# Row maxima spread by one bf16 matmul, raw weights of a block in one tile, and loads and sums of the next chunk tied elsewhere in an attention and FFN kernel

## The chip, the cores and the metric

The kernel runs on one core of a Trainium2 chip. The metric is the device time of one execution in microseconds (us). The kernel before was timed three times: 1032.73, 1033.56 and 1032.63 us, a median of 1032.73 us.

## The reference

Windowed causal attention with a linear bias per head, and behind it a feed-forward network (FFN) on all tokens; q and k come in multiplied by 8:

```python
# q, k, v: 8 batches, 8 heads, 576 positions, 64 numbers; float32
scores = scale * np.matmul(q, k.transpose(0, 1, 3, 2))          # scale = 1/8
bias = slopes[:, None, None] * (-np.abs(rel).astype(np.float32))[None, :, :]
mask = (rel >= 0) & (rel < window)                               # window = 128
attn = softmax(np.where(mask, scores + bias[None], -1e9))
x = np.matmul(attn, v)                  # then heads side by side: 4608 tokens x 512
h = x @ w_in                            # 512 x 2048
g = np.where(h >= 1, h, np.where(h <= -1, 0.0, (h + 1) ** 2 / 4.0))
return g @ w_out                        # 2048 x 512
```

`w_in` and `w_out` are float64; the kernel gets them as pairs of 32-bit words and makes float32 of them itself.

## The kernel before

**Tiling.** The 4608 tokens go in 12 chunks of 384 (`CH`), three blocks of 128 each. In a chunk the 8 heads are 4 pairs, so that there are 48 pairs; pair p belongs to chunk p // 4. Chunks 0 and 1 (`c < LIGHT`) have float32 attention, one head after the other (`scores`, `weights_t`, `values`). Chunks from 2 on have it in split fp16: each float32 operand becomes a high and a low half (ACT makes the high one, DVE the low one: `split_qk` L367/L368, `split_v` L424/L425), and three products replace one (`scores_of_pair` L453, `values_of_pair` L557). The FFN of a chunk has 16 blocks fc of 128 hidden units: `layer1` is 12 fp16 matmuls of 384 columns (L585 to L587), `layer2` 9 of 512 columns (L616 to L618; in chunk 0 three in float32, L613). Between the two ACT (L592, L601), DVE (L593, L594) and POOL (L602) make the quadratic unit and its two halves.

**Scales.** A split needs a scale made of the greatest absolute value over a whole tensor. Each engine row (partition) first has its own maximum or sum. To take the maximum over the 128 partitions, `spread` lets POOL multiply a 128x128 identity by that column (L152), a float32 matmul with a matrix of ones turns the diagonal into 128 equal rows (L157), and DVE takes the maximum along the row (L159) and makes scale and inverse (L162 to L170). That happens 19 times: `m_i0` to `m_i15` for the blocks of `w_in`, `m_x0` and `m_x1` for v of chunks 0 and 1, `m_o` for all of `w_out`. For chunks 2 to 11, `level` and `scale_all` do it for two columns at once: POOL L335 twice, one float32 matmul of 256 columns, L341. A float32 matmul is issued as two passes, which is why the profile counts 32 `m_i` and 20 `m`.

**Weights.** Block fc of `w_in` and of `w_out` arrives in two raw tiles (`rawi`, `rawo`, three of each) by two DMAs on ACT's queue. `float32_of` makes float32 of each: ACT scales the high words (L176) and the low words (L177), DVE shifts (L178) and adds (L179). `convert_in` has the row maximum `rows_i` made behind it (L198), `convert_out` a sum (L222). Three blocks are converted in the attention of chunk 0, the others in its FFN, three blocks ahead of their use.

**Loads and sums of a pair.** From pair 8 on `load_all(p)` brings q, k and v by DMAs on SP's queue. q and k of pairs from 12 on go into one of five tiles in turn (`p % 5`, taken over from the raw weights), v into one of six (`vn`). `reach_of(p)` makes the row maximum of v on DVE (L384, `rows<-vn`) and the sums of the absolute values of q and of k on ACT (L318, `junk<-qk`); when a chunk's four pairs have theirs, `level` and `scale_all` make the chunk's scales, on which `split_qk` of its first pair waits.

**The order.** The attention is a list of `segments`, the FFN a list of its own; of the first so many are emitted after each half of an FFN block that the attention of chunk c + 1 lies in the FFN of chunk c. A scheduler then orders each engine's instructions, by dependences and a simulated time. `behind(instructions, f)` asks that what f emits stand behind the named instructions; it orders instructions of the same engine only. In each turn p of the loop at the end of the list there are, in this order:

```python
reach_of(p + 4); scores_of_pair(p, (0, 1)); level(c + 1)   # level: last pair of a chunk
scores_of_pair(p, (2,)); split_v(p); values_of_pair(p - 1)
scale_all(c + 1)                                           # last pair of a chunk
weights_t(2 * p); split_qk(p + 1) and load_all(p + 5); weights_t(2 * p + 1)
```

Of the kernel before, what the change touches and what calls it, by code (L numbers as in the profile page):

```python
# [20 lines left out]
def windowed_attention_then_ffn(  # L21
# [83 lines left out]
    for m in range(H):  # L105
# [8 lines left out]
    G.affine_select(out=rel, in_=rel, pattern=[[-1, 2 * P]], base=P, channel_multiplier=1,  # L114
                    compare_op=ALU.is_ge, fill=NEG)

    sums = const.tile([P, 2, NQB, 2], F32, name="sums")
    G.memset(sums, 1.0e-9)

# [12 lines left out]
            G.memset(t[:D, 1], 0.0)  # L132


    ones = const.tile([P, P], F32, name="ones")
    G.memset(ones, 1.0)
# [11 lines left out]

    def spread(name, rows):

        diag[name] = ap1.tile([P, P], F32, name=f"d_{name}", tag="d", bufs=2)
        G.tensor_scalar(diag[name], ident, rows, None, ALU.mult)  # L152

    def scale_of(name, s, i):

        b = bank(f"m_{name}")[:, :P]
        T.matmul(b, ones, diag.pop(name), start=True, stop=True)  # L157
# [11 lines left out]
    def float32_of(w, name, out=None):

        low, high = w[..., 0], w[..., 1]
        f = stg.tile([P] + list(w.shape[1:-1]), F32, name=f"f_{name}", tag="stg")
        fi = f.bitcast(I32)


        S.activation(high.bitcast(F32), high.bitcast(F32), AF.Prelu, scale=2.0 ** -112, alpha=2.0 ** 32)  # L176
        S.activation(low, low.bitcast(U32), AF.Copy, scale=2.0 ** -29)  # L177
        V.tensor_scalar(fi, high, 3, None, ALU.logical_shift_left)  # L178
        V.tensor_tensor(fi if out is None else out.bitcast(I32), fi, low, ALU.add)  # L179
        return f  # L180

    raw = {}

    def fetch_weights(fc):
        w1 = rawp.tile([P, NCC, P, 2], I32, name=f"rawi{fc}", tag=f"rawi{fc % 3}")
        S.dma_start(w1, wi32[:, 2 * fc * P:2 * (fc + 1) * P].rearrange("(c p) (f w) -> p c f w", p=P, w=2))

        w2 = rawp.tile([P, DM, 2], I32, name=f"rawo{fc}", tag=f"rawo{fc % 3}")
        S.dma_start(w2, wo32[fc * P:(fc + 1) * P, :].rearrange("p (f w) -> p f w", w=2))
        raw[fc] = (w1, w2)  # L190

    wide = {}

    def convert_in(fc):
        f = wide[fc] = wp.tile([P, NCC, P], F32, name=f"f_i{fc}", tag="f_i", bufs=3)
        float32_of(raw[fc][0], f"i{fc}", out=f)
        rows = column(f"rows_i{fc}", "rows")
        V.tensor_reduce(rows, f.rearrange("p c f -> p (c f)"), X, ALU.max, apply_absolute_value=True)  # L198
# [9 lines left out]
    def split_in(fc):  # L208
        if fc > 1:
            fall_in(fc)  # L210
        f, s1 = wide.pop(fc), s_in[:, fc:fc + 1]
        t = wi[fc] = wp.tile([P, 2, NCC, P], F16, name=f"wi{fc}", tag=f"wi{fc}")
# [5 lines left out]

    def convert_out(fc):
        wf[fc] = wp.tile([P, DM], F32, name=f"wf{fc}", tag=f"wf{fc}")  # L220
        float32_of(raw[fc][1], f"o{fc}", out=wf[fc])
        S.activation(junk, wf[fc], AF.Abs, accum_out=rows_o[:, fc:fc + 1])  # L222

    def scale_out(stage):
# [56 lines left out]
    def load_qk(p):  # L281
# [9 lines left out]
        for j, r in enumerate(lo_rows):  # L291
            DMA.dma_start(kr[r, j, :n], k[g * P + j * D:g * P + (j + 1) * D, (c + 1) * CH - n:(c + 1) * CH])

    def load_all(p):

        c, g = divmod(p, NPAIR)
        n = CH + before(c) * P
        if c == LIGHT:
            t = wp.tile([P, 2 * CH + P], F32, name=f"qk_{p}", tag=f"wo{NPAIR + g}")
        else:  # L300
            tag = ("rawi0", "rawi1", "rawi2", "rawo0", "rawo1")[p % 5]
            t = rawp.tile([P, 2 * CH + P], F32, name=f"qk_{p}", tag=tag)
# [17 lines left out]
    def level(c):  # L320

        rq, rk = tops.pop((c, "q")), tops.pop((c, "k"))
        iq, t = column(f"i_q{c}", "i_q", n=NPAIR), column(f"t{c}", "t", n=NPAIR)
        top = column(f"tt{c}", "tt", n=2)
        s_q[c], s_k[c] = column(f"s_q{c}", "s_q", n=NPAIR), column(f"s_k{c}", "s_k", n=NPAIR)
        V.tensor_scalar(iq.bitcast(I32), rq.bitcast(I32), 0x7F800000, None, ALU.bitwise_and)
        V.tensor_scalar(iq, iq, 2.0 ** -60, 1.0 / TOP, ALU.max, ALU.mult)
        V.reciprocal(s_q[c], iq)
        V.tensor_tensor(iq, iq, qscale, ALU.mult)
        V.tensor_tensor(t, rk, iq, ALU.mult)  # L330
        V.tensor_reduce(top[:, 0:1], t, X, ALU.max)
        V.tensor_reduce(top[:, 1:2], tops.pop(c)[:, :NPAIR], X, ALU.max)
        d = diag[c] = ap1.tile([P, 2, P], F32, name=f"d_{c}", tag="qr")
        for a in range(2):
            G.tensor_scalar(d[:, a], ident, top[:, a:a + 1], None, ALU.mult)  # L335
        tops[c, "i"] = iq

    def scale_all(c):

        b = bank(f"m_{c}")[:, :2 * P]  # L340
        T.matmul(b, ones, diag.pop(c).rearrange("p a w -> p (a w)"), start=True, stop=True)  # L341
# [11 lines left out]
        if "t" not in rels:  # L353
            rels["t"] = rawp.tile([P, NQB, 2 * P], F32, name="rels", tag="rawo2")
        rels[c] = rels["t"][:, c % 2], rels["t"][:, 2]
# [87 lines left out]
    def scores_of_pair(p, blks):  # L443
# [191 lines left out]
    for m in range(M1):  # L635
# [9 lines left out]
        if m >= 2:  # L645
            part["e"] = [[lambda m=m: values(m - 2)]]
        if odd:
            part["v"] = [[lambda p=p: load_v(p + 4)]] if p < NPAIR else []
            part["v"] += [[lambda x=x: load_all(x)] for x in {5: (8, 9), 6: (10,), 7: (11,)}.get(p, ())]
# [14 lines left out]
    for p in range(M1 // 2, NP):  # L664
        c, g = divmod(p, NPAIR)
        new = p + NPAIR < NP
        if new:
            segments.append([lambda p=p: reach_of(p + NPAIR)])
        segments.append([lambda p=p: scores_of_pair(p, (0, 1))])
        if new and g == NPAIR - 1:  # L670
            segments.append([lambda c=c: level(c + 1)])
        segments.append([lambda p=p: scores_of_pair(p, (2,))])
        segments.append([lambda p=p: split_v(p)])
        if p > M1 // 2:
# [6 lines left out]
        segments.append(([lambda p=p: split_qk(p + 1)] if p + 1 < NP else []) + ([lambda p=p: load_all(p + 5)] if p + 5 < NP else []))  # L681
# [129 lines left out]
```

## Time and profile before

| | |
|---|---|
| median of three runs | 1032.73 us |
| the profiled execution | 1030.51 us |
| its span in the profile | 1028.3 us |
| mean granted TensorE clock | 0.979 |
| instructions in the span | 17951 |

The span runs from the first to the last instruction of the profiled execution; 2.2 us of that execution lie outside it, and the execution itself is 2.2 us below the median. PE is TensorE's matmuls, PEld its weight loads, DVE VectorE, ACT ScalarE, POOL GpSimd, SP the queue that issues loads and stores. A group of instructions reads: line, engine, operation, tiles written and read, shapes, count, then busy time in us and the mean of one in ns, then idle time of the engine ahead of them and what released it. The chain is followed back from the last instruction to whatever released each step.

### The profile page before, as it was taken

How to read it: one execution, taken by the hardware profiler on the slowest of the kernel's cores; microseconds unless marked ns; L12 is line 12 of the kernel's file. 1: busy time of each engine (PE TensorE's matmuls, PEld its weight loads, DVE VectorE, ACT ScalarE, POOL GpSimd, SP SyncE). 2: the span in 40 equal slices, each digit the busy share in tenths (PEclk: the TensorE clock that was granted, in tenths of full speed). 3: DMA queues.
4: the chain of work that ended last, by engine and by line, in shares of the span. 5: the costliest groups of instructions: out<-in, count | busy, mean ns of one | idle time of the engine just before them, and what ended most of it. 6: DMA issues, size and time to landing. Idle time of an engine off the chain costs nothing.

```text
span 1028.3 us, 17951 instructions
## 1 busy us (share of the span) xinstructions
PE 975.1 (95%) x6218; PEld 548.8 (53%) x6218; DVE 742.2 (72%) x2128; ACT 618.2 (60%) x1547; POOL 374.7 (36%) x479
## 2 busy tenths in 40 slices
PE   7579999997899899899999999999999999999998
PEld 7446554554455455455555555555555555555554
DVE  5789889887767677777777777777777867775322
ACT  4678878665756655655755765765755755654332
POOL 5332211334344323433433433433434434334221
PEclk9889999999799999999999999999999999999999
DMA  8445442002101101201211201111101100000000
GB/s 258 159 154 168 160 142 85 1 11 73 52 22 57 57 24 35 69 30 39 68 40 40 74 24 47 57 30 57 60 29 57 50 2 1 32 1 1 32 1 31
DMA packets 53275, 59.88 MB, mean 58 GB/s; under 512 B 3520, under 2 KB 42432, under 8 KB 53184
## 3 DMA queue, kind: packets, MB, share of 16 engines
q1 hardware_dynamic: 42432, 41.96, 13.0%
q10 hardware_dynamic: 10752, 16.78, 4.8%
q8 instruction: 49, 0.80, 0.3%
q14 instruction: 42, 0.34, 0.1%
HBM read 49.28 MB, written 9.44 MB: 57 GB/s over the span
## 4 chain that ended last, share of the span: by engine, by line
PE 81%; DVE 8%; DMA 4%; ACT 3%; issue 2%; POOL 1%; ACTq 0%; SPq 0%; DVEq 0%; POOLq 0%
PE h L585 11%; PE h L587 11%; PE h L586 11%; PE acc L616 11%; PE acc L617 11%; PE acc L618 11%; PE s L453 5%; PE x L557 4%; PE p L497 3%; DMA vn<-in_v_dram 2%; PE acc L613 2%; PE x L536 1%; DVE g L593 1%; ACT z L478 1%; DVE g L594 1%
## 5 line engine op out<-in xcount | busy, mean ns | idle before, releaser
L602 POOL TENSOR_TENSOR gl<-g,gh 128x384 f16<-128x384 f32 x176 | 164.8, 936 | 394.1 <-ACT gh L601 375.9
L593 DVE SCALAR_TENSOR_TENSOR g<-u,half 128x384 f32<-128x384 f32 x176 | 121.0, 689 | 178.1 <-ACT u L592 167.9
L616 PE MATMUL acc<-wo,gh 128*128 128x512 f16 x528 | 200.0, 380 | 0.4 <-ACT wo L238 0.4
L617 PE MATMUL acc<-wo,gh 128*128 128x512 f16 x528 | 200.3, 379 | 0.0
L618 PE MATMUL acc<-wo,gl 128*128 128x512 f16 x528 | 197.0, 379 | 0.0
L601 ACT CAST gh<-g 128x384 f16<-128x384 f32 x176 | 89.7, 509 | 177.3 <-DVE g L594 124.7
L592 ACT ACTIVATE u<-h,shift,fall 128x384 f32<-128x384 f32 x176 | 116.4, 664 | 88.9 <-PE h L587 88.2
L478 ACT ACTIVATE z<-z,nmax 128x256 f32<-128x256 f32 (+2 forms) x288 | 137.7, 479 | 35.5 <-DVE nmax L476 34.8
L585 PE MATMUL h<-xh,wi 128*128 128x384 f16 x448 | 146.4, 328 | 3.7 <-DVE g L594 3.7
L587 PE MATMUL h<-xh,wi 128*128 128x384 f16 x448 | 147.4, 329 | 1.3 <-DVE wi L214 1.3
L586 PE MATMUL h<-xl,wi 128*128 128x384 f16 x448 | 147.2, 328 | 0.0
L476 DVE CUSTOM_DVE_ANT_0 z<-s,rels,z_of 128x256 f32<-128x256 f32 (+2 forms) x240 | 98.4, 459 | 26.8 <-PE s L453 26.4
L594 DVE SCALAR_TENSOR_TENSOR g<-h,gain,g 128x384 f32<-128x384 f32 x176 | 107.8, 614 | 3.8
L585 PE MATMUL h<-x,wi 128*128 128x384 f16 x320 | 105.3, 331 | 4.4 <-ACT x L566 3.1
L586 PEld LDWEIGHTS <-wi 128*128 128x128 f16 x768 | 75.7, 99 | 62.2 <-issue 9.2
L585 PEld LDWEIGHTS <-wi 128*128 128x128 f16 x768 | 75.5, 98 | 62.1 <-issue 6.6
L586 PE MATMUL h<-x,wi 128*128 128x384 f16 x320 | 105.9, 331 | 0.2 <-DVE x L567 0.2
L587 PE MATMUL h<-x,wi 128*128 128x384 f16 x320 | 105.9, 331 | 0.0
L587 PEld LDWEIGHTS <-wi 128*128 128x128 f16 x768 | 75.7, 99 | 54.6 <-issue 4.2
L512 POOL TENSOR_SCALAR_AFFINE_SELECT lu<-lu 128x768 f16<-128x768 f16 x80 | 72.5, 914 | 71.0 <-DVE lu L510 56.7
L618 PEld LDWEIGHTS <-gl 128*128 128x128 f16 x528 | 51.5, 98 | 58.6 <-issue 1.1
L616 PEld LDWEIGHTS <-gh 128*128 128x128 f16 x528 | 51.6, 98 | 52.0 <-issue 2.2
(154 smaller groups left out, 1555.4 us busy)
## 6 DMA issues: line engine op xcount, KB each, us to landing
out_dram<-o SPq DMA_DIRECT2D x36, 256.0 KB, 2.1
rawi<-in_moe_w_in_dram ACTq DMA_DIRECT2D x16, 512.0 KB, 3.7
rawo<-in_moe_w_out_dram ACTq DMA_DIRECT2D x16, 512.0 KB, 4.7
vn<-in_v_dram SPq DMA_DIRECT2D x32, 256.0 KB, 3.0
qk<-in_q_dram SPq DMA_DIRECT2D x40, 192.0 KB, 3.0
qk<-in_k_dram SPq DMA_DIRECT2D x28, 256.0 KB, 3.5
vn<-in_v_dram SPq DMA_DIRECT2D x16, 192.0 KB, 2.7
qk<-in_k_dram SPq DMA_DIRECT2D x12, 192.0 KB, 2.8
```

What stands on the lines that cost most here:

```text
L476: V.tensor_tensor_reduce(out=z[:, i, c0:], in0=pt[:, n, c0:], in1=r[:, c0:], op0=ALU.add, op1=ALU.min, scale=factor, scalar=3.0e38, accum_ ...
L478: S.activation(z[:, i, c0:], z[:, i, c0:], AF.Exp, bias=nmax[:, i:i + 1], scale=-1.0, accum_out=sm[:, i, 0:1])
L585: T.matmul(ph, wi[fc][:, 0, cc, :], xh, start=(cc == 0), stop=False)
L586: T.matmul(ph, wi[fc][:, 0, cc, :], xl, start=False, stop=False)
L587: T.matmul(ph, wi[fc][:, 1, cc, :], xh, start=False, stop=(cc == NCC - 1))
L592: first = S.activation(u, ph, AF.Relu, bias=shift[c] if c else quarter, scale=fall[c][:, col])
L593: V.scalar_tensor_tensor(g, u, half[c] if c else 0.5, u, ALU.min, ALU.mult)
L594: last = V.scalar_tensor_tensor(g, ph, gain[c][:, col] if c else fall[c][:, col], g, ALU.mult, ALU.max)
L602: G.tensor_tensor(gl, g, gh, ALU.subtract)
L616: T.matmul(a, gh[:, ts], wo[fc][:, 0], start=first, stop=False)
L617: T.matmul(a, gh[:, ts], wo[fc][:, 1], start=False, stop=False)
L618: T.matmul(a, gl[:, ts], wo[fc][:, 0], start=False, stop=last)
```

## The change

1. **Spreading a row maximum.** `spread` and `level` make no diagonals any more, they only keep the column. `across` (new) issues one bf16 matmul of 128 columns for each column: the weights are the upper 16 bits of the column, read 128 times over with a stride of zero, and the moving operand is a bf16 identity, which POOL copies once at the start in place of the `ones`. The maximum is only used through its exponent.
2. **Raw weights.** A block's two halves have one tile `raw` (three in turn), by the same two DMAs. `unfold` runs ACT once over the high words of both halves and once over the low words (128x1024 each), in `convert_in`; `float32_of` is one DVE instruction for a half, a shift and an or (L192 after), without a temporary tile.
3. **Six lasting halves.** q and k of pairs from 12 on go to `two[p // 2 % 3][:, p % 2]`, three tiles allocated once with two halves each, in place of five tiles in turn. The scaled distances (`rels`) have a constant tile `near` of their own, one set in place of two in turn.
4. **Turn of a pair.** `load_all(p + 5)` stands at the head of turn p, as a segment of its own, no longer behind `split_qk(p + 1)`; `reach_of(p + 4)` stands behind the first scores and is tied by `behind` to their last matmul. `load_v` and `load_all` of the first chunks are tied to `done_t`, which holds instructions of DVE, ACT and POOL.

```diff
     def spread(name, rows):
-        diag[name] = ap1.tile([P, P], F32, name=f"d_{name}", tag="d", bufs=2)
-        G.tensor_scalar(diag[name], ident, rows, None, ALU.mult)
+        diag[name] = rows
+
+    def across(b, rows):
+        r = rows.bitcast(BF16)
+        for a in range(rows.shape[1]):
+            T.matmul(b[:, a * P:(a + 1) * P], r[:, 2 * a + 1:2 * a + 2].broadcast_to([P, P]), ident16, start=True, stop=True)
...
-        T.matmul(b, ones, diag.pop(name), start=True, stop=True)
+        across(b, diag.pop(name))
...
-        S.activation(low, low.bitcast(U32), AF.Copy, scale=2.0 ** -29)
-        V.tensor_scalar(fi, high, 3, None, ALU.logical_shift_left)
-        V.tensor_tensor(fi if out is None else out.bitcast(I32), fi, low, ALU.add)
-        return f
...
+    def unfold(fc, which=slice(0, 2)):
+        low, high = raw[fc][:, which, :, 0], raw[fc][:, which, :, 1]
         S.activation(high.bitcast(F32), high.bitcast(F32), AF.Prelu, scale=2.0 ** -112, alpha=2.0 ** 32)
+        S.activation(low, low.bitcast(U32), AF.Copy, scale=0.9375 * 2.0 ** -29)
+
+    def float32_of(fc, a, out):
+        V.scalar_tensor_tensor(out.bitcast(I32), raw[fc][:, a, :, 1], 3, raw[fc][:, a, :, 0], ALU.logical_shift_left, ALU.bitwise_or)
...
     def convert_in(fc):
-        f = wide[fc] = wp.tile([P, NCC, P], F32, name=f"f_i{fc}", tag="f_i", bufs=3)
-        float32_of(raw[fc][0], f"i{fc}", out=f)
+        f = wide[fc] = wp.tile([P, DM], F32, name=f"f_i{fc}", tag="f_i", bufs=3)
+        unfold(fc)
+        float32_of(fc, 0, f)
...
     def load_all(p):
-            tag = ("rawi0", "rawi1", "rawi2", "rawo0", "rawo1")[p % 5]
-            t = rawp.tile([P, 2 * CH + P], F32, name=f"qk_{p}", tag=tag)
+            i = p // 2 % 3
+            if i not in two:
+                two[i] = rawp.tile([P, 2, 2 * CH + P], F32, name=f"qk_{p}", tag=f"raw{i}")
+            t = two[i][:, p % 2]
...
-        d = diag[c] = ap1.tile([P, 2, P], F32, name=f"d_{c}", tag="qr")
-        for a in range(2):
-            G.tensor_scalar(d[:, a], ident, top[:, a:a + 1], None, ALU.mult)
+        diag[c] = top
...
+        if p + 5 < NP:
+            segments.append([lambda p=p: load_all(p + 5)])
+        segments.append([lambda p=p: scores_of_pair(p, (0, 1))])
         if new:
-            segments.append([lambda p=p: reach_of(p + NPAIR)])
-        segments.append([lambda p=p: scores_of_pair(p, (0, 1))])
+            segments.append([lambda p=p: behind([head[2 * p]["scored"]], lambda: reach_of(p + NPAIR))])
```

**Three places in the order.** First DVE in the attention of chunk 0, where block 2 of `w_in` is converted: `f_i2` is its float32, `rows_i2` its row maximum, `rows_2<-vn_9` the row maximum of v of pair 9, for which a DMA must have landed. Before:

```order
L179 ISA f_i2_634<-rawi2_347,f_i2_635 128x1024
L489 TENSOR_TENSOR ep_8_605<-z_8_606,rc_8_617 128x384
L384 TENSOR_REDUCE rows_2_1261<-vn_9_961 128x1
L198 TENSOR_REDUCE rows_i2_640<-f_i2_634 128x1
L484 TENSOR_REDUCE rc_9_665<-sums_129 128x3
```

DVE at the same place after:

```order
L192 SCALAR_TENSOR_TENSOR f_i2_612<-raw2_346 128x512
L192 SCALAR_TENSOR_TENSOR wf2_658<-raw2_346 128x512
L218 SCALAR_TENSOR_TENSOR wi1_661<-f_i1_447,s_in_153,wi1_661 128x512
L201 TENSOR_REDUCE rows_i2_616<-f_i2_612 128x1
L388 TENSOR_REDUCE rows_2_1166<-vn_9_902 128x1
```

`rows_i2` has moved ahead of the instruction that waits for the DMA, and the block's `w_out` half is converted ahead of both.

Second ACT at the boundary of chunks 2 and 3, where the first pairs of chunk 3 (pairs 12 to 14) are split into `h` and the sums of chunk 4 (`rows_q4`, `rows_k4`) are made; `z_24` and `z_25` are the exponentials of pair 12. Before, with the pair in the tile's name:

```order
L367 ACTIVATE h_12_2698<-qk_12_1721,s_k3_2520 128x384
L367 ACTIVATE h_13_2930<-qk_13_2001,s_k3_2520 128x384
L318 ACTIVATE junk_158,rows_q4_2728<-qk_17_2935 128x384
L318 ACTIVATE junk_158,rows_k4_2729<-qk_17_2935 128x512
L478 ACTIVATE z_24_2771,sums_129<-z_24_2771,nmax_24_2772 128x128
L478 ACTIVATE z_24_2771,sums_129<-z_24_2771,nmax_24_2772 128x256
L318 ACTIVATE junk_158,rows_q4_2728<-qk_18_3178 128x384
L478 ACTIVATE z_25_2778,sums_129<-z_25_2778,nmax_25_2779 128x128
L478 ACTIVATE z_25_2778,sums_129<-z_25_2778,nmax_25_2779 128x256
L367 ACTIVATE h_14_3173<-qk_14_2216,s_q3_2519 128x384
L367 ACTIVATE h_14_3173<-qk_14_2216,s_k3_2520 128x384
L318 ACTIVATE junk_158,rows_k4_2729<-qk_18_3178 128x512
```

ACT there after, where `qk_12` is the lasting tile of pairs 12, 13, 18 and 19, and `qk_14` that of 14, 15, 20 and 21:

```order
L371 ACTIVATE h_12_2547<-qk_12_1571,s_k3_2371 128x384
L371 ACTIVATE h_13_2778<-qk_12_1571,s_k3_2371 128x384
L326 ACTIVATE junk_159,rows_k4_2629<-qk_12_1571 128x512
L483 ACTIVATE z_24_2613,sums_130<-z_24_2613,nmax_24_2614 128x128
L326 ACTIVATE junk_159,rows_q4_2628<-qk_12_1571 128x384
L483 ACTIVATE z_24_2613,sums_130<-z_24_2613,nmax_24_2614 128x256
L483 ACTIVATE z_25_2620,sums_130<-z_25_2620,nmax_25_2621 128x128
L326 ACTIVATE junk_159,rows_k4_2629<-qk_12_1571 128x512
L483 ACTIVATE z_25_2620,sums_130<-z_25_2620,nmax_25_2621 128x256
L371 ACTIVATE h_14_3020<-qk_14_1874,s_q3_2370 128x384
L371 ACTIVATE h_14_3020<-qk_14_1874,s_k3_2371 128x384
```

The sums of pair 17 have gone from here to an earlier place, and those of the remaining pairs still stand right behind the splits that free their buffers, the first of them ahead of all of `z_24`.

Third DVE at the same boundary, where `level` of chunk 4 works on those sums (`i_q4`, `s_q4`, `t4`). Before:

```order
L489 TENSOR_TENSOR ep_24_2770<-z_24_2771,rc_24_2803 128x384
L425 SCALAR_TENSOR_TENSOR vs_14_3316<-vn_14_2219,s_23_2645,vs_14_3316 128x384
L489 TENSOR_TENSOR ep_25_2777<-z_25_2778,rc_25_2810 128x384
L326 TENSOR_SCALAR i_q4_3494<-rows_q4_2728 128x4
L327 TENSOR_SCALAR i_q4_3494<-i_q4_3494 128x4
L593 SCALAR_TENSOR_TENSOR g_2_0_2972<-u_2_0_2971,half2_2917 128x384
```

DVE there after:

```order
L340 TENSOR_REDUCE tt4_3363<-rows_4_2626 128x1
L334 TENSOR_SCALAR i_q4_3361<-rows_q4_2628 128x4
L335 TENSOR_SCALAR i_q4_3361<-i_q4_3361 128x4
L481 ISA z_25_2620,nmax_25_2621<-s_25_2_2642,near_129,z_of3_2496 128x256
L481 ISA nmax_25_2621 128x1
L336 RECIPROCAL s_q4_3364<-i_q4_3361 128x4
L481 ISA z_24_2613,nmax_24_2614<-s_24_2_2641,near_129,z_of3_2496 128x256
```

`level` has moved up from behind the pair's probabilities (`ep`) to between its scores, ahead of the last two `z` of the pair.

More of the change, by code (lines that the diff above doesn't have):

```diff
@@ L115, in windowed_attention_then_ffn @@
                     compare_op=ALU.is_ge, fill=NEG)
+    near = const.tile([P, 2, 2 * P], F32, name="near")
     sums = const.tile([P, 2, NQB, 2], F32, name="sums")
@@ L132, in windowed_attention_then_ffn @@
             G.memset(t[:D, 1], 0.0)
-    ones = const.tile([P, P], F32, name="ones")
-    G.memset(ones, 1.0)
+    ident16 = const.tile([P, P], BF16, name="ident16")
+    G.tensor_copy(ident16, ident)
     s_in = const.tile([P, NFC], F32, name="s_in")
@@ L167, in windowed_attention_then_ffn @@
     wo32 = w_out.bitcast(I32)
[L169 to L176, printed above, removed]
-        S.activation(low, low.bitcast(U32), AF.Copy, scale=2.0 ** -29)
-        V.tensor_scalar(fi, high, 3, None, ALU.logical_shift_left)
-        V.tensor_tensor(fi if out is None else out.bitcast(I32), fi, low, ALU.add)
-        return f
     raw = {}
     def fetch_weights(fc):
[L185 to L190, printed above, removed]
+        w = raw[fc] = rawp.tile([P, 2, DM, 2], I32, name=f"raw{fc}", tag=f"raw{fc % 3}")
+        S.dma_start(w[:, 0].rearrange("p (c f) w -> p c f w", c=NCC),
+                    wi32[:, 2 * fc * P:2 * (fc + 1) * P].rearrange("(c p) (f w) -> p c f w", p=P, w=2))
+        S.dma_start(w[:, 1], wo32[fc * P:(fc + 1) * P, :].rearrange("p (f w) -> p f w", w=2))
+    def unfold(fc, which=slice(0, 2)):
+        low, high = raw[fc][:, which, :, 0], raw[fc][:, which, :, 1]
+        S.activation(high.bitcast(F32), high.bitcast(F32), AF.Prelu, scale=2.0 ** -112, alpha=2.0 ** 32)
+        S.activation(low, low.bitcast(U32), AF.Copy, scale=0.9375 * 2.0 ** -29)
+    def float32_of(fc, a, out):
+        V.scalar_tensor_tensor(out.bitcast(I32), raw[fc][:, a, :, 1], 3, raw[fc][:, a, :, 0], ALU.logical_shift_left, ALU.bitwise_or)
     wide = {}
     def convert_in(fc):
-        f = wide[fc] = wp.tile([P, NCC, P], F32, name=f"f_i{fc}", tag="f_i", bufs=3)
-        float32_of(raw[fc][0], f"i{fc}", out=f)
+        f = wide[fc] = wp.tile([P, DM], F32, name=f"f_i{fc}", tag="f_i", bufs=3)
+        unfold(fc)
+        float32_of(fc, 0, f)
         rows = column(f"rows_i{fc}", "rows")
-        V.tensor_reduce(rows, f.rearrange("p c f -> p (c f)"), X, ALU.max, apply_absolute_value=True)
+        V.tensor_reduce(rows, f, X, ALU.max, apply_absolute_value=True)
         spread(f"i{fc}", rows)
@@ L211, in split_in @@
         f, s1 = wide.pop(fc), s_in[:, fc:fc + 1]
-        t = wi[fc] = wp.tile([P, 2, NCC, P], F16, name=f"wi{fc}", tag=f"wi{fc}")
+        t = wp.tile([P, 2, DM], F16, name=f"wi{fc}", tag=f"wi{fc}")
+        wi[fc] = t.rearrange("p s (c f) -> p s c f", c=NCC)
         S.activation(t[:, 0], f, AF.Copy, scale=s1)
@@ L220, in convert_out @@
         wf[fc] = wp.tile([P, DM], F32, name=f"wf{fc}", tag=f"wf{fc}")
-        float32_of(raw[fc][1], f"o{fc}", out=wf[fc])
+        float32_of(fc, 1, wf[fc])
         S.activation(junk, wf[fc], AF.Abs, accum_out=rows_o[:, fc:fc + 1])
@@ L292, in load_qk @@
             DMA.dma_start(kr[r, j, :n], k[g * P + j * D:g * P + (j + 1) * D, (c + 1) * CH - n:(c + 1) * CH])
+    two = {}
     def load_all(p):
@@ L340, in scale_all @@
         b = bank(f"m_{c}")[:, :2 * P]
-        T.matmul(b, ones, diag.pop(c).rearrange("p a w -> p (a w)"), start=True, stop=True)
+        across(b, diag.pop(c))
         i_2[c], s_2[c] = column(f"i_2{c}", "i_2", 3, 2), column(f"s_2{c}", "s_2", 3, 2)
@@ L352, in scale_all @@
         V.tensor_scalar(z_of[c], fade, i_2[c][:, 0:1], None, ALU.mult)
-        if "t" not in rels:
-            rels["t"] = rawp.tile([P, NQB, 2 * P], F32, name="rels", tag="rawo2")
-        rels[c] = rels["t"][:, c % 2], rels["t"][:, 2]
+        rels[c] = near[:, 0], near[:, 1]
         V.tensor_scalar(rels[c][0], rel, s_2[c][:, 0:1], -1.0e38, ALU.mult, ALU.max)
@@ L457, in scores_of_pair @@
             soften(2 * p + j, blks, pts[j])
+            head[2 * p + j]["scored"] = last[0]
     def soften(m, blks, pt):
@@ L647, in windowed_attention_then_ffn @@
         if odd:
-            part["v"] = [[lambda p=p: load_v(p + 4)]] if p < NPAIR else []
-            part["v"] += [[lambda x=x: load_all(x)] for x in {5: (8, 9), 6: (10,), 7: (11,)}.get(p, ())]
+            part["v"] = [[lambda p=p: behind(done_t[2 * p], lambda: load_v(p + 4))]] if p < NPAIR else []
+            part["v"] += [[lambda p=p, x=x: behind(done_t[2 * p - 1], lambda: load_all(x))] for x in {5: (8, 9), 6: (10,), 7: (11,)}.get(p, ())]
             part["v"] += [[lambda x=x: reach_of(x)] for x in {3: (4, 5), 4: (6, 7), 6: (8,), 7: (9,)}.get(p, ())]
@@ L663, in windowed_attention_then_ffn @@
     segments += [[lambda: load_all(p8 + 4)], [lambda: scale_all(LIGHT)], [lambda: split_qk(p8)]]
-    for p in range(M1 // 2, NP):
+    for p in range(p8, NP):
         c, g = divmod(p, NPAIR)
         new = p + NPAIR < NP
+        if p + 5 < NP:
+            segments.append([lambda p=p: load_all(p + 5)])
+        segments.append([lambda p=p: scores_of_pair(p, (0, 1))])
         if new:
-            segments.append([lambda p=p: reach_of(p + NPAIR)])
-        segments.append([lambda p=p: scores_of_pair(p, (0, 1))])
+            segments.append([lambda p=p: behind([head[2 * p]["scored"]], lambda: reach_of(p + NPAIR))])
         if new and g == NPAIR - 1:
@@ L673, in windowed_attention_then_ffn @@
         segments.append([lambda p=p: split_v(p)])
[L674 removed]
+        if p > p8:
             segments.append([lambda p=p: values_of_pair(p - 1)])
@@ L680, in windowed_attention_then_ffn @@
         segments.append([lambda p=p: weights_t(2 * p)])
-        segments.append(([lambda p=p: split_qk(p + 1)] if p + 1 < NP else []) + ([lambda p=p: load_all(p + 5)] if p + 5 < NP else []))
+        if p + 1 < NP:
+            segments.append([lambda p=p: split_qk(p + 1)])
         segments.append([lambda p=p: weights_t(2 * p + 1)])
```

## The prediction

> **What bounds the kernel now.** I read the table by windows first, to see in which stages TensorE has nothing to do. Its columns are the window, its length, then busy us (and count) of PE, PEld, DVE, ACT and POOL, the granted clock, the DMA share and GB/s:
>
> ```profile
> 0.00:180.00 180.00, 149.36 (x722) 97.19 (x723) 147.92 (x489) 131.68 (x324) 54.87 (x105) 0.95 0.51 161
> 240.00:280.00 40.00, 28.78 (x202) 15.84 (x201) 29.24 (x103) 25.93 (x74) 12.74 (x14) 0.79 0.24 75
> 320.00:360.00 40.00, 37.10 (x225) 19.65 (x222) 29.08 (x86) 25.33 (x63) 16.91 (x21) 0.96 0.23 73
> 400.00:440.00 40.00, 36.42 (x243) 19.56 (x244) 32.02 (x101) 27.45 (x71) 14.66 (x17) 0.96 0.21 67
> 440.00:1000.00 560.00, 560.00 (x3758) 307.40 (x3756) 392.45 (x1085) 319.58 (x807) 214.92 (x253) 1.00 0.11 35
> ```
>
> From 440 to 1000 us PE is busy for all 560.00 us: there only matmul time counts, and whatever DVE, ACT or POOL saves is worth nothing. In the first 180 us PE stands idle for 30.64 us, and at three boundaries between chunks for 11.22, 2.90 and 3.58 us, 17.7 us together. So the change can gain in two ways: matmul time anywhere, and waits in the first 180 us and at those boundaries.
>
> What PE waits for in the first 180 us is in the list of waits for that window (engine, line, what it waited for; total, times, longest):
>
> ```profile
> PE p L497 <- DVE rc L484: 7.4, 1, 7.4
> PE m_i L157 <- POOL d_i L152: 6.8, 5, 3.2
> ...
> PE m_x L157 <- POOL d_x L152: 3.4, 2, 2.1
> ```
>
> The second and the third, 10.2 us, are the matmuls that spread a row maximum, waiting for the diagonal that POOL makes. What lies behind such a wait shows in the chain of waits for the window (start, length, piece):
>
> ```profile
> 22.57 7.44 DMA vn<-in_v_dram
> ...
> 31.18 0.60 DVE f_i L179
> ...
> 37.14 0.70 PE m_i L157 x2
> ...
> 54.36 4.78 DMA vn<-in_v_dram
> 59.16 0.69 DVE rows L384
> 59.84 0.59 DVE rows_i L198
> 60.61 1.47 POOL d_i L152
> ...
> 127.92 0.78 POOL d_i L152
> 128.74 0.49 PE m_i L157 x2
> ...
> 139.12 0.60 DVE f_i L179
> ```
>
> Here and in its left-out lines the chain holds six POOL diagonals, 6.13 us in all (those shown are the first and the last), eight matmul pieces of L157, 3.79 us (first and last shown), and 20 pieces of the shift and the add, L178 and L179, 9.8 us (first and last shown).
>
> **The change part by part.** The spreading first. The six diagonals leave the chain: -6.1 us. Nothing takes their place but the row maximum itself, on which POOL had waited. The matmul becomes one bf16 pass of 128 columns. The trace has no such matmul with stride-zero weights; the nearest pieces of the chain are those of transposes in float32 and of fp16 scores, with two pieces of the boundary that I need below:
>
> ```profile
> 193.63 0.66 PE p L497 x6
> ...
> 198.88 0.76 PE s L453 x12
> ...
> 254.00 3.46 DMA qk<-in_k_dram
> ...
> 262.24 2.46 DMA qk<-in_q_dram
> ```
>
> A float32 pass of 128 columns is 0.66 / 6 = 0.11 us, a pass of fp16 0.76 / 12 = 0.063 us. I take 0.063 for the new pass, as the nearest in type; 0.11 is the upper end. The eight pieces on the early chain then go from 3.79 to 0.5 us, -3.3 us. The ten matmuls of a chunk's scales go from two passes of 256 columns, 4 x 0.11 = 0.44 us, to two of 0.063: -0.31 us each, -3.1 us, and that is PE time, kept where nothing waits too. The upper end gives -2.2.
>
> Block 2 of `w_in` gains by its place: in the chain above its row maximum stood on DVE behind `rows`, which waited 4.78 us for v of pair 9. The order has it ahead of that instruction now. What is late next is the rest of that time's work on DVE and ACT; I take -2 us, between 0 and -4.78.
>
> PE's clock is part of that place, and of the boundary:
>
> ```profile
> 64.00:66.00 2.00, 1.59 (x5) 0.44 (x3) 1.07 (x7) 0.76 (x3) 0.00 (x0) 0.50 0.17 31
> 258.00:262.00 4.00, 2.48 (x28) 1.82 (x25) 2.20 (x10) 4.00 (x16) 0.60 (x1) 0.50 0.11 36
> ```
>
> Behind both pauses the granted clock is 0.50, so that the matmuls take twice as long. If the pause ahead of 64 us becomes short enough, 1.59 us of matmuls there become 0.8; this is inside the 2 us. The Trainium skill, page "TensorE: Matmul & The Clock Gate", Part 1, says that the clock has only two states and falls to half after an idle window of about 3.4 us; the 0.50 agrees, and by that rule a pause cut to below the window wins the whole stretch at once, so the end of -4.78 would be the likelier one.
>
> The conversion of the weights is the second part. These are the groups of its instructions, and of the nearest to the new one:
>
> ```profile
> L239 DVE SCALAR_TENSOR_TENSOR wo<-wf,s_out,wo 128x512 f16<-128x512 f32 x16 | 11.7, 741 | 0.0
> ...
> L179 DVE CUSTOM_DVE_ANT_0 f_i<-rawi,f_i 128x1024 uint16<-128x1024 uint16 x16 | 11.0, 688 | 0.0
> L176 ACT ACTIVATE rawi<-rawi 128x512 f32<-128x512 f32 x16 | 10.8, 678 | 4.8 <-DMA kz<-in_k_dram 2.8 <-issue 1.2 <-ACT lu L501 0.6
> ...
> L178 DVE TENSOR_SCALAR f_i<-rawi 128x512 int32<-128x512 int32 x16 | 6.8, 423 | 0.3 <-ACT rawi L176 0.3
> ```
>
> Shift and add are 0.423 + 0.688 = 1.11 us for a half. The one instruction that replaces them reads two tensors of 32 bits as L239 does, 0.741 us; the ends are 0.423, as the shift alone, and 1.11, no gain. I take 0.741, a third off: of the chain's 9.8 us -3.3. The Trainium skill, page "VectorE: DVE Perf Modes", section "What auto-detection actually checks", speaks against more: an operation with two sources has a faster mode for 16-bit data only, so that one instruction in place of two does not halve the time; from its figures for N elements I estimate (512 + 8 + 150) / 0.96 GHz = 0.70 us, by which the term would be -3.6. The rows agree: 0.423 with one source, 0.741 with two.
>
> On ACT four instructions of 0.678 us become two of twice the length, each between 0.678 and 1.36 us; by the length I take the upper half of that. The total hardly changes, but the `w_in` half now waits until both halves are scaled, up to 1.36 us longer per block. ACT is busy for 131.68 of the first 180 us and runs ahead of DVE at most blocks, which hides it; if that cover is gone, it is paid at some of 16 blocks. I take +1 us, with ends at 0 and +10. Together the conversion gives -2.3.
>
> The early terms make -6.1 - 3.3 - 2 - 2.3 = -13.7 us. Some of it runs into the next late thing: the 7.4 us of the transpose behind the DMA of v, at the same place of the order before and after, stays, and so do PE's own product matmuls. I keep three quarters, -10.3 us, which is also what PE's two waits for POOL (10.2 us) allow.
>
> Loads and sums are the third part. The boundary at 250 us pays for two DMAs on the chain, 3.46 and 2.46 us: ACT reaches the sums of a pair just loaded, `junk<-qk`, and everything behind it on ACT (the exponentials `z`, the splits `h`, the `u` of the FFN) stands in the queue. The change means those sums to stand behind the scores. The tie names a matmul, while the sums are ACT instructions and the v maximum is one of DVE; the ties of the loads name DVE, ACT and POOL, while the loads are on SP. So these ties move nothing, and in the order the sums still stand right behind the splits that free their buffers. What does change: the pair is one turn earlier (the sums of pair 17 have left the boundary), and on SP's queue the q loads of pairs 18 and 19 stand ahead of the two v loads, while k still stands behind them, which wait for the split of v. I take -3 us for the boundaries, nearest to the shorter of the two DMAs, with ends of -6 (both gone) and +6 (both twice as long).
>
> The freed POOL time, the dropped `ones` and the constant `near` cost nothing: PE waits for none of them after 180 us.
>
> The sum is -10.3 - 3.1 - 3 = -16.4 us. The span of 1028.3 becomes 1011.9, the profiled execution of 1030.51 becomes 1014.1, and since that lay 2.2 us below the median, I forecast 1016 us.
>
> **The rivals.** *Only the matmul passes count.* The wait for POOL becomes a wait for the same row maximum on DVE, which is the busiest engine next to PE in this stage (147.92 of 180 us). Then 3.1 + 3.3 us are gained: 1026 us. The 4.78 us of DMA ahead of the row maximum speak for it; against it, POOL's 0.78 to 1.47 us stand between the two as pieces of their own.
>
> *The boundaries go.* If loads a turn ahead mean that no sum finds its data missing, the 17.7 us at the three boundaries are won and not 3: 1001 us. The earlier load speaks for it. The order speaks against it, with the sum of k right behind the split that frees its buffer.
>
> *Slower: DVE waits ahead of the scores.* `level` now stands on DVE between the scores of a chunk's last turn, ahead of the last two `z` of the pair; it waits for ACT's sums, and these for a DMA. The longest such wait is in the list of waits:
>
> ```profile
> ACT junk L318 <- DMA qk<-in_q_dram: 43.1, 23, 4.5
> ```
>
> If DVE waits 4.5 us at each of the nine boundaries and PE has nothing queued, 40 us come on top, 1056 us; with half of it covered 1036 us. It decides where the wait outlasts the FFN matmuls queued on PE. Against it: 23 such waits on ACT, 43.1 us in all, leave PE busy for 560.00 of 560 us after 440.
>
> *No change.* The gains of the first 180 us are eaten by the later `w_in` halves and the boundaries: 1031 to 1034 us.
>
> **How the numbers follow.** I give my forecast 0.58 (its own range 1007 to 1024), the matmul passes alone 0.17, the boundaries 0.12, the slower case 0.08, no change 0.05. About 0.2%, 2 us, is what a measurement of this kernel can tell from no change. So faster has 0.58 + 0.17 + 0.12 = 0.87, the same 0.05, slower 0.08. The range goes from 1000, where the boundaries go, to 1029, which holds the matmul passes alone with the upper end of the new pass; it leaves out the slower case, no change and the outer ends.
>
> **What would show it.** Right: no PE wait for POOL `d` in the first 180 us, PE busy there for a larger share, that stage some 10 us shorter; one pass per spread matmul; the new DVE group near 0.74 us; PE still busy for the whole of its time from chunk 5 on; stalls of ACT `junk` behind DMAs still there at the first boundaries. Wrong: PE idle after 440 us, or DVE `i_q` waiting for ACT `junk` for several us at each boundary (slower), or PE never idle at 250 us (boundaries gone).

## The result and the profile after

The changed kernel takes 1037.01 us (median of 20 runs, 1033.28 to 1042.32) against 1029.14 us for the kernel before in as many runs (1025.01 to 1034.7): a ratio of 1.0078, 95% interval 1.0061 to 1.0096. It is slower by 8 us where 16 us less were forecast, and lies outside the range. The kernel before is faster here than in the three runs from which the forecast started (1032.73 us). The profiled execution of the changed kernel took 1035.11 us, with a span of 1033.4 us. One of the twelve executions of the kernel before beside e1 to e4 took 5630.9 us and is left out of their ratios.

The same five windows as before show where to look (window, length, busy us of PE, PEld, DVE, ACT and POOL, granted clock, DMA share, GB/s):

```profile
0.00:180.00 180.00, 153.09 (x757) 98.55 (x758) 149.46 (x480) 136.86 (x311) 36.69 (x84) 0.97 0.51 163
240.00:280.00 40.00, 29.75 (x189) 16.34 (x189) 29.75 (x91) 24.18 (x67) 14.54 (x16) 0.79 0.21 64
320.00:360.00 40.00, 36.50 (x238) 19.56 (x233) 28.35 (x83) 25.99 (x68) 12.38 (x17) 0.96 0.16 51
400.00:440.00 40.00, 37.27 (x256) 20.21 (x255) 32.73 (x88) 26.88 (x69) 15.76 (x17) 1.00 0.23 72
440.00:1000.00 560.00, 546.24 (x3664) 298.14 (x3663) 385.02 (x1064) 312.74 (x787) 205.11 (x240) 0.99 0.11 33
```

In the first 180 us PE runs 35 matmuls more than before. The last row is the surprise: where PE had been busy for 560.00 of 560 us it now stands idle for 13.76 us, and the clock falls below 1.00. The waits of PE, first in the window up to 180 us, then from 440 to 1000 us:

```profile
PE p L502 <- DVE rc L490: 5.6, 1, 5.6
...
PE acc L618 <- DVE g L599: 3.2, 3, 1.6
...
PE p L502 <- DVE rc L489: 2.4, 1, 2.4
PE p L502 <- DVE ep L494: 2.1, 2, 1.9
...
PE h L590 <- ACT xh L583: 1.6, 2, 1.4
PE h L591 <- DVE xl L584: 1.1, 1, 1.1
...
PE m_i L159 <- DVE rows_i L201: 0.7, 1, 0.7
```

```profile
PE h L590 <- DVE g L599: 12.1, 6, 3.3
```

The 10.2 us of waits for POOL diagonals are gone, and PE waits only 0.7 us for the row maximum. But other waits have come, for DVE's `rc` (L489) and `ep` and for the halves of x: up to the start of chunk 1's FFN products PE is idle for 26.91 us, against 30.66 us before. And six times after 440 us the first layer now waits for DVE's `g`, 12.1 us in all.

To see where time is won and lost, here is the start of the first second-layer matmul of some FFN blocks (`acc`, L616 before, L621 after), in us for the kernel before and as a difference to it for the others. The runs e1 to e9 are those of the next section.

| chunk, block | before | after | e1 | e2 | e3 | e4 | e5 | e6 | e8 | e9 |
|---|---|---|---|---|---|---|---|---|---|---|
| 1, 0 | 180.02 | -10.84 | -1.75 | -5.64 | +0.15 | -11.96 | -8.23 | -10.33 | -5.84 | -0.47 |
| 2, 4 | 290.87 | -10.14 | -9.69 | -5.28 | +1.15 | -18.55 | -6.25 | -14.07 | -6.33 | -0.97 |
| 4, 4 | 454.35 | -12.90 | -11.96 | -8.01 | +2.84 | -26.73 | -15.97 | -25.85 | -8.41 | -2.74 |
| 6, 4 | 606.75 | -5.60 | -4.09 | -8.07 | +4.57 | -23.34 | -14.51 | -27.05 | -1.25 | +0.75 |
| 8, 4 | 759.72 | +1.07 | +2.80 | -8.81 | +5.32 | -21.03 | -15.25 | -28.14 | +6.63 | +7.06 |
| 11, 8 | 998.03 | +5.14 | +9.16 | -9.13 | +6.50 | -16.14 | -14.65 | -28.85 | +11.18 | +13.43 |

Each column is one profiled execution. In e2, e5 and e7 (not in the table) every engine runs the order of the changed kernel up to 224 us, and yet they are 5.64, 8.23 and 8.92 us ahead in the first row: differences of some 5 us between single entries of that row show nothing.

The changed kernel is 10.84 us ahead when chunk 1's FFN begins and 12.90 us ahead in chunk 4. Then it loses 18 us, at one chunk boundary after the other. One such boundary, that of chunks 5 and 6, in the chain of waits (start, length, piece):

```profile
570.57 3.08 DMA qk<-in_q_dram
...
573.73 0.62 ACT junk L326 x2
...
575.47 0.68 ACT o L626
576.15 0.57 ACT u L597
576.72 0.02 issue
576.74 0.59 DVE g L598
577.33 0.04 issue
577.38 0.62 DVE g L598
577.99 0.54 DVE g L599
578.53 0.04 issue
578.57 0.48 PE h L590
579.05 0.32 PE h L591
```

ACT reaches the sums of a pair whose q has not landed, then writes outputs, and only then makes the new chunk's first `u`; DVE makes `g` of it, and PE, which has no matmul left, waits for that `g` for 3.3 us. Before, PE was never without work there. What differs is the order on ACT. Before, behind the boundary's last split of v:

```order
L424 ACTIVATE vs_30_7314<-vn_30_6185,s_27_6624 128x512
L592 ACTIVATE u_5_15_6892<-h_5_15_6879,shift5_5923,fall5_4631 128x384
L318 ACTIVATE junk_158,rows_q8_6727<-qk_35_7391 128x384
L318 ACTIVATE junk_158,rows_k8_6728<-qk_35_7391 128x512
L601 CAST gh_5_15_6897<-g_5_15_6893 128x384
L592 ACTIVATE u_6_0_6959<-h_6_0_6946,shift6_6906,fall6_5638 128x384
```

After, from the last FFN block of chunk 5 on:

```order
L597 ACTIVATE u_5_15_6716<-h_5_15_6703,shift5_5753,fall5_4468 128x384
L606 CAST gh_5_15_6721<-g_5_15_6717 128x384
L371 ACTIVATE h_30_6992<-qk_12_1571,s_q7_6349 128x384
...
L428 ACTIVATE vs_30_7136<-vn_30_5812,s_27_6449 128x512
L326 ACTIVATE junk_159,rows_q9_7604<-qk_12_1571 128x384
L326 ACTIVATE junk_159,rows_k9_7605<-qk_12_1571 128x384
L626 ACTIVATE o_5_0_6880<-acc_5_0_5963,o_g5_5751 128x512
```

The last FFN block of the old chunk (`u_5_15`, `gh_5_15`) has slipped ahead of the boundary's last attention work. On PE the same slip shows. Before, the first layer of block 15 ends behind the last product of attention, `x_27`, and 27 second-layer matmuls of the old chunk are still to come behind that product. After, block 15 is done ahead of `x_27`, 18 are left, and they are spent before the new chunk's first `g` is there.

That count, taken from the traces at every boundary, goes with the stalls. At the boundaries from chunks 4/5 to 9/10 the kernel before has 25 to 34 second-layer matmuls left and no stall; after has 12 to 22, and PE stops at each for 0.83 to 3.30 us. The kernel before has the slipped phase too, at the boundaries of chunks 2/3 and 3/4: 19 and 9 are left there, and these are the places of its stalls of 2.90 and 3.58 us near 340 and 420 us.

### The profile page after: what moved, and what is told of

Read it like the earlier page. It is cut to its first block, busy times and chain, and to the rows that moved or that the text cites. A ratio compares the mean times of both kernels' runs of the same rounds, so it can differ in the third digit from the quotient of the medians.

```text
span 1033.4 us, 17799 instructions
## 1 busy us (share of the span) xinstructions
PE 970.4 (94%) x6199; PEld 543.8 (53%) x6199; DVE 736.9 (71%) x2096; ACT 616.4 (60%) x1515; POOL 344.9 (33%) x440
## 4 chain that ended last, share of the span: by engine, by line
PE 65%; DVE 17%; ACT 7%; DMA 6%; issue 3%; POOL 1%; ACTq 0%; SPq 0%; DVEq 0%; POOLq 0%
PE h L590 9%; PE h L592 9%; PE h L591 9%; PE acc L621 8%; PE acc L622 8%; PE acc L623 8%; PE s L457 4%; DVE g L598 3%; DMA qk<-in_k_dram 3%; PE x L562 3%; DMA vn<-in_v_dram 2%; ACT z L483 2%; DVE h L372 2%; PE p L502 2%; DVE g L599 2%
## 5 line engine op out<-in xcount | busy, mean ns | idle before, releaser
L598 DVE SCALAR_TENSOR_TENSOR g<-u,half 128x384 f32<-128x384 f32 x176 | 124.1, 707 | 184.9 <-ACT u L597 173.3
L621 PE MATMUL acc<-wo,gh 128*128 128x512 f16 x528 | 200.3, 380 | 0.0
L481 DVE CUSTOM_DVE_ANT_0 z<-s,near,z_of 128x256 f32<-128x256 f32 (+2 forms) x240 | 98.5, 459 | 33.9 <-PE s L457 33.6
L621 PEld LDWEIGHTS <-gh 128*128 128x128 f16 x528 | 51.5, 98 | 53.3 <-issue 2.1
```

Source lines behind the costliest of these rows:

```text
L481: V.tensor_tensor_reduce(out=z[:, i, c0:], in0=pt[:, n, c0:], in1=r[:, c0:], op0=ALU.add, op1=ALU.min, scale=factor, scalar=3.0e38, accum_ ...
L598: V.scalar_tensor_tensor(g, u, half[c] if c else 0.5, u, ALU.min, ALU.mult)
L621: T.matmul(a, gh[:, ts], wo[fc][:, 0], start=first, stop=False)
```

## The experiments

Two theories at first. **P, the phase**: what costs is that the FFN's last block stands ahead of the next chunk's last attention work, whatever brought that about. **H, the sixth half**: with six halves the sums at a boundary are those of a later pair, and their DMA is what costs.

**e1: the spreading alone, in the kernel before.** Five tiles, old weights, old turn.

```diff
-        diag[name] = ap1.tile([P, P], F32, name=f"d_{name}", tag="d", bufs=2)
-        G.tensor_scalar(diag[name], ident, rows, None, ALU.mult)
+        diag[name] = rows
...
-        T.matmul(b, ones, diag.pop(name), start=True, stop=True)
+        across(b, diag.pop(name))
```

> The kernel before with the bf16 spreading alone (five tiles in turn, two raw tiles, old turn of a pair). Its order has, as after, the last FFN block of a chunk (u, gh) ahead of the boundary's last scores on ACT, and two sums directly ahead of the next chunk's first u. Theory P (the phase between FFN and attention slipped by one FFN block, whatever brought it; each boundary from 490 us on then costs 2 to 6 us): some 7 us won in the first 180 us, PE idle again after 440 us for 8 to 18 us as after, so between 3 us faster and 10 us slower than before. Theory H (the sixth half is what costs, since sums of a later pair stand at the boundary): 6 to 9 us faster than before, PE idle under 2 us after 440 us.

Measured: 1038.77 us against 1029.72 us, ratio 1.0077 (1.0054 to 1.0101). The window from 440 us and PE's longest waits in it:

```profile
440.00:1000.00 560.00, 544.24 (x3647) 296.45 (x3646) 382.47 (x1064) 311.99 (x790) 205.75 (x239) 0.99 0.11 34
```

```profile
PE h L588 <- DVE g L597: 15.2, 6, 4.0
```

With five tiles and none of the new loads, the stalls are there (15.76 us of idle PE): H falls as the sole cause.

**e2: the change with five halves in place of six.**

```diff
-            i = p // 2 % 3
+            i = p % 5 // 2
...
-            t = two[i][:, p % 2]
+            t = two[i][:, p % 5 % 2]
```

> The kernel after with five lasting halves in turn in place of six. Its order has the last FFN block behind the boundary's last split of v on ACT, as before. Theory P: the 10 us of the first stage stay and PE is idle under 3 us after 440 us: 9 to 14 us faster than before. Theory H: the same, 9 to 14 us faster. If it is no faster than after, both fall.

Measured: 1019.95 us, ratio 0.9902 (0.9871 to 0.9934), 10 us faster than before.

```profile
440.00:1000.00 560.00, 559.58 (x3763) 306.28 (x3762) 388.92 (x1077) 317.34 (x801) 208.87 (x245) 1.00 0.11 34
```

PE is idle for 0.42 us there, as the order without the slip says. By itself this fits both theories; with e1 it does not speak for H. In its first stage 5.64 us are won, less than the 10 us that both theories kept, though the order there is that of the change.

**e3: six tiles alone, in the kernel before.**

```diff
-            tag = ("rawi0", "rawi1", "rawi2", "rawo0", "rawo1")[p % 5]
+            tag = ("rawi0", "rawo0", "rawi1", "rawo1", "rawi2", "rawo2")[p % 6]
...
-        rels[c] = rels["t"][:, c % 2], rels["t"][:, 2]
+        rels[c] = near[:, 0], near[:, 1]
```

> The kernel before with six tiles in turn for q and k in place of five, and the scaled distances in a constant tile. Its order keeps the last FFN block behind the last split of v, but the sums at the boundary are those of a pair later, as after. Theory P: within 3 us of before, PE idle under 2 us after 440 us. Theory H: 12 to 18 us slower than before, PE idle 10 us or more after 440 us.

Measured: 1035.53 us, ratio 1.0048 (1.0024 to 1.0072), some 5 us slower: more than P allowed, well under what H asked for. PE is idle for 2.35 us after 440 us (557.65 of 560 busy) and for 19.90 us from 180 to 440 us, where it was 17.71 us before; the table shows the loss in steps of about a microsecond over many boundaries. So the sixth tile, or the constant tile that came with it, costs something of its own; why is not settled.

**e4: the sums tied to their own engines.** The change's tie names a matmul, which orders neither ACT nor DVE. Here the sums stand behind the exponential of the pair's first scores, the maximum of v behind their reduction.

```diff
-behind([head[2 * p]["scored"]], lambda: reach_of(p + NPAIR))
+behind([head[2 * p + 1]["exp"].ins, head[2 * p + 1]["red"].ins], lambda: reach_of(p + NPAIR))
```

> The kernel after with the sums tied to instructions of their own engines: ACT's sums behind the exponential of the pair's first scores, DVE's maximum behind the scores' reduction. In its order no sum stands directly ahead of a next chunk's first u any more; sums lie one at a time between other work, a turn after their load. Theory P with the cause of the price in the sums ahead of u: the early 10 us stay and the boundary stalls after 440 us go (under 4 us), those at 250, 340 and 420 us shrink too: 10 to 25 us faster than before. Theory H: the sixth half is still there, but the tie undoes its effect, so also faster, 8 to 14 us, with the stalls at 250, 340 and 420 us as they are. If phase alone counts (u and gh of the last block ahead of the boundary) and not the sums, PE stays idle some 12 us after 440 us and it is within 5 us of after.

Measured: 1013.87 us, ratio 0.9847 (0.9819 to 0.9874), 16 us faster than before. The table has 26.73 us won in chunk 4: the boundaries at 250, 340 and 420 us have shrunk as well. But PE still waits from 440 us on, at most 1.8 us at a time:

```profile
PE h L590 <- DVE g L599: 8.7, 6, 1.8
```

Neither theory's expectation holds whole: P asked for under 4 us of idle PE after 440 us, and it is 8.68; H asked for the early stalls as they were. ACT's waits for q and k at the sums, 57 us over the whole run in the change (30.6 for k, 26.6 for q), are all gone, and still PE stops at each boundary. So the price seems to have two parts: the sums and their DMA ahead of the new chunk's `u`, which this tie takes away, and the slipped phase, which it leaves. e5 and e6 try that.

**e5: the phase put back by one tie on PE.** Six halves and the sums as in the change.

```diff
+            elif 0 < c < NCHUNK - 1 and fc == NFC - 1:
+                ops.append(lambda c=c, fc=fc: behind([last_x[0]], lambda: layer1(c, fc)))
```

Here `last_x` is the last product matmul of the next chunk's attention. The theory set against P here is S: the sums cost, whatever the phase.

> The kernel after with one tie more, on PE: the first-layer matmuls of a chunk's last FFN block stand behind the last product matmul (x) of the next chunk's attention. Six halves and the sums where after has them; in its order the last block's u and gh stand behind the boundary's last split of v again. Theory P (the slipped phase is what costs): PE idle under 3 us after 440 us, the 10 us of the first stage kept: 8 to 14 us faster than before. Theory S (the sums ahead of the next chunk's work, whatever the phase, since six halves make ACT wait for a later pair): as after, 5 to 9 us slower than before. If the tie itself makes PE wait for x, PE shows waits at h of block 15 and it lies between.

Measured: 1015.04 us, ratio 0.9849 (0.9828 to 0.987), 16 us faster than before, more than the 8 to 14 of theory P, and some 23 us faster than the change by the two ratios.

```profile
440.00:1000.00 560.00, 558.08 (x3742) 305.09 (x3740) 390.51 (x1067) 314.39 (x788) 205.42 (x240) 1.00 0.10 33
```

```profile
PE p L502 <- DVE shift L412: 1.1, 2, 0.6
```

The waits of `h` for `g` are gone, though ACT waits for the loads as it did: over the whole run its waits for q and k are 23.7 + 27.2 us, against 26.6 + 30.6 us in the change and 43.1 + 2.4 us before. Behind the tie PE has 23 to 32 second-layer matmuls left at the boundaries from 4/5 to 8/9, in place of 12 to 22, and from 440 us on it is idle for 1.92 us only.

**e6: both ties.** The edits of e4 and e5 together, in the change.

> The kernel after with both ties, the sums' (as in the run before with its own engines) and PE's. Theory P: the 8.7 us of waits after 440 us that the sums' tie alone left are the phase's, and go: 22 to 28 us faster than before, some 1003 us, PE idle under 2 us after 440 us. Theory S: the sums' tie took all that sums cost, what is left is the latency of a new chunk's first u, g, and no tie changes it: within 3 us of the sums' tie alone, 13 to 18 us faster than before.

Measured: 999.74 us, ratio 0.9702 (0.9679 to 0.9725), 31 us faster than before, more than the 22 to 28 of theory P, and the best of all. From 440 us to 980 us (the window ends earlier, since its span ends at 999.4 us):

```profile
440.00:980.00 540.00, 540.00 (x3636) 296.24 (x3635) 384.39 (x1056) 312.53 (x788) 202.24 (x237) 1.00 0.11 34
```

That speaks for P: the 8.7 us that the sums' tie left were the phase's. With the sums out of the way 18 to 23 second-layer matmuls are enough here; with the sums in the way, as in the change, PE stopped at 18 and at 22.

**e7: the turn of a pair as before, in the change.** The load goes back behind `split_qk`, `reach_of` ahead of the scores, without a tie.

```diff
-            segments.append([lambda p=p: load_all(p + 5)])
...
-            segments.append([lambda p=p: behind([head[2 * p]["scored"]], lambda: reach_of(p + NPAIR))])
+            segments.append([lambda p=p: reach_of(p + NPAIR)])
```

> The kernel after with the turn of a pair as before: the load behind the next pair's split, the sums ahead of the scores, no tie. Its order is that of after on every engine up to the last pairs. All theories in which the emitted order of a turn does not reach the engines: as after, 5 to 9 us slower than before. If the earlier load or the tie did anything, it differs from after by over 3 us.

Measured: 1034.98 us, ratio 1.006 (1.003 to 1.009), as the change: the new turn did nothing to the engines, whose instructions come in the same order in both traces up to 930 us. PE's wait after 440 us is the same one:

```profile
PE h L590 <- DVE g L599: 12.4, 6, 3.5
```

**e8: the change with POOL's diagonals kept.**

```diff
-        across(b, diag.pop(name))
+        T.matmul(b, ones, diag.pop(name), start=True, stop=True)
```

> The kernel after with POOL's diagonals and the float32 matmuls kept: the raw weights in one tile, six halves and the new turn alone. The first stage shows what the conversion gives by itself: 2 to 4 us by the prediction's terms at the first product of chunk 1, against 10.8 in after. Its order has the slipped phase at the boundaries from chunk 4 on, so by theory P PE is idle 8 to 15 us after 440 us and it is 3 to 14 us slower than after. If the slip comes from the bf16 spreading, PE is idle under 3 us there.

Measured: 1044.22 us, ratio 1.0131 (1.0104 to 1.0158). The first stage is 5.84 us shorter without the spreading, where 2 to 4 were expected; with one execution of each that is no clear difference. The slip is there too, with 14.8 us of idle PE after 440 us: it is no property of the bf16 spreading.

```profile
PE h L593 <- DVE g L602: 13.3, 6, 4.2
```

**e9: the slip alone, in the kernel before.** One number of the pacing; nothing of the change is in it.

```diff
-            emit_attention(int(now + (end - now) * (r + (4 if c else 7)) / STEPS))
+            emit_attention(int(now + (end - now) * (r + (2 if c else 7)) / STEPS))
```

> The kernel before with one number changed: its attention is emitted two half-blocks of the FFN later (the 4 in the pacing becomes 2). Nothing of the change is in it: diagonals, five tiles, old weights, old turn. In its order the last product matmul of the next chunk stands behind the first-layer matmuls of a chunk's last FFN block at the boundaries from chunk 4 on, and the last block's u and gh ahead of the boundary's last scores on ACT, as in after. Theory P: PE is idle 8 to 18 us after 440 us and it is 8 to 18 us slower than before. If the slip needs the six halves, the freed POOL or the new sums to cost anything, it is within 3 us of before.

Measured: 1045.18 us, ratio 1.0144 (1.0094 to 1.0194).

```profile
440.00:1000.00 560.00, 549.39 (x3671) 299.34 (x3668) 384.04 (x1069) 317.46 (x795) 213.30 (x250) 0.99 0.11 35
```

```profile
PE h L585 <- DVE g L594: 7.3, 4, 2.3
PE s L453 <- DVE lu L510: 3.3, 1, 3.3
```

So the slip costs about as much in a kernel that has none of the change's parts: PE is idle for 10.61 us there, 7.3 us of it at the wait that the change has too, and 3.3 us at another behind the same slip. It stops where 9 to 21 second-layer matmuls are left, and not at the two boundaries, 4/5 and 7/8, where 26 are left. P is shown from both sides: put in (e9), taken out (e5, e6), and present or absent with the order in e1, e2, e7 and e8.

## Why the prediction was wrong

**The first stage was right in sum, in part by luck.** Forecast -10.3 us, measured -10.84 us at the start of chunk 1's FFN products. Three other executions of the same order give -5.64, -8.23 and -8.92 us there. Nor is it won as I said: PE's waits for POOL, 10.2 us, went, but PE is idle for only 3.75 us less (26.91 us against 30.66), since other late work took their place. The other 7.1 us are time in which PE is busy (142.27 us against 149.36), of cheaper passes and of a clock of 0.97 against 0.95 in the first 180 us; it is 0.94 and 0.95 in those other executions. How the gain divides among the parts is not shown: e8, without the spreading, has 5.84 us where the terms of the conversion had 2.3, and e1, the spreading alone, has 1.75 us there and 9.69 us by chunk 2, each in one execution.

**The prices of single instructions were right.** At each of the ten chunk scales the two bf16 passes hold PE for 0.11 us in place of 0.43, the -3.1 us of the sum. For the conversion these are the new groups on ACT and DVE:

```profile
L187 ACT ACTIVATE raw<-raw 128x1024 f32<-128x1024 f32 x16 | 18.5, 1156 | 4.3 <-DMA kz<-in_k_dram 3.3 <-ACT lu L506 0.6 <-issue 0.4
L188 ACT ACTIVATE raw<-raw 128x1024 int32<-128x1024 uint32 x16 | 18.2, 1137 | 0.0
...
L192 DVE SCALAR_TENSOR_TENSOR wf<-raw 128x512 int32<-128x512 int32 x16 | 12.2, 762 | 0.0
...
L192 DVE SCALAR_TENSOR_TENSOR f_i<-raw 128x512 int32<-128x512 int32 x16 | 11.0, 688 | 1.0 <-ACT raw L188 0.7
```

I took 741 ns from L239 for the merged instruction and between 0.678 and 1.36 us for ACT's. My estimate of 0.70 us by the two-source rule of the Trainium skill's page "VectorE: DVE Perf Modes", section "What auto-detection actually checks", lies between the two measured means. DVE waits for ACT's scaled halves for 0.7 us in all, where the sum has 1.

**The early boundaries gave nothing that shows.** Forecast -3 us. From 180 to 440 us PE is idle for 17.57 us, against 17.71 us before. The lead does grow from 9.3 to 12.9 us between chunk 1, block 8 (203.37 us against 212.69) and chunk 4, block 4, but at the later place the changed kernel has 12 score matmuls still to do that the kernel before had done, and e1, without the new loads, grows its lead to 11.96 us. That the tie of the sums moves nothing was right (e7); the ties of the first chunks' loads were not tried by themselves.

**The step that failed** is the one that the whole of the rest stood on: "From 440 to 1000 us PE is busy for all 560.00 us: there only matmul time counts". That is a fact of the order of the kernel before, and I carried it over to another order, so that the boundaries after 440 us stood in the sum with nothing. In the new order PE is idle for 13.76 us there, 12.1 us of it where the first layer waits for `g`. The cover consisted of the second-layer matmuls that PE still held when the new chunk's first `u` was late, 25 to 34 before and 12 to 22 after. I compared the orders at the boundary of chunks 2 and 3, where both have the same phase, the slipped one, and not at a boundary after 440 us, where the slip could be read in a few rows.

**The slower rival had the sign and the stage, not the mechanism.** It let DVE wait in `level` ahead of the scores. That wait is 2.7 us in all after 440 us:

```profile
DVE i_q L334 <- ACT junk L326: 2.7, 5, 0.8
```

Its price was 20 to 40 us, and that its milder time of 1036 us meets the measured one is luck. What I held against it, 43.1 us of ACT waits that PE never felt, was again the old order's cover; besides, those 43.1 us are of the whole run, and 28.0 us of them lie after 440 us. The loads a turn ahead, which the term of the boundaries and a rival took as a gain, come with the sixth half; e3, which has it with the constant tile and no other part, is some 5 us slower.

What brings the slip about in the change stays open. It was only read: the scheduler orders each engine by a simulated time, and e1, e8 and the change, which shorten different parts of the early work, come out with it, while e2 and e3 come out without.

## What to carry to other kernels

A stage without a wait is covered by what the order leaves queued, and a change far away can spend that cover when a scheduler makes the order anew: compare the two orders where each stage hands over to the next, above all in the stages that show no wait. If a phase matters, write it down as a tie between instructions of the same engine; one such tie on the matmuls turned a loss of 8 us into a gain of 16 us, and one for the sums on their own engines made it 31 us. A tie to an instruction of another engine orders nothing here.

## What the runs showed of the hardware

A stall of 3.3 us on PE costs more than its length. Behind the one that ends at 578.57 us the granted clock is low, and a first-layer matmul takes 0.32 us in the chain, as against 0.16 us at 583.63 us:

```profile
578.00:582.00 4.00, 3.43 (x11) 1.57 (x11) 2.22 (x6) 1.63 (x4) 2.80 (x4) 0.57 0.17 66
659.00:663.00 4.00, 3.46 (x18) 1.61 (x19) 1.94 (x4) 1.26 (x3) 2.98 (x4) 0.68 0.00 0
```

The second row is the boundary of chunks 6 and 7, behind a wait of 3.16 us. The Trainium skill's page "TensorE: Matmul & The Clock Gate", Part 1, puts the fall to half clock at an idle window of about 3.4 us; the half agrees (0.50 in the second row below), the length only roughly. In e1 a pause of 3.08 us, up to 660.96 us, is followed by no fall, and one of 2.10 us, up to 740.16 us, by 3.4 us at half clock:

```profile
661.00:664.40 3.40, 3.40 (x26) 1.83 (x26) 1.82 (x4) 1.64 (x3) 2.96 (x4) 1.00 0.00 0
741.11:744.52 3.41, 3.41 (x13) 1.67 (x11) 1.16 (x4) 1.26 (x3) 3.35 (x5) 0.50 0.22 79
```

Of the 18 us that the change lost after chunk 4, 13.76 us are idle PE, and for the other 4.3 us PE is busy longer than before. The matmuls at the lower clock behind the two stalls above are part of that; the rest was not divided up.
